# Sending the probabilities of eight head pairs through DRAM instead of TensorE's transposes, with single token tiles and a later branch, in a kernel of attention and two expert layers

## The chip, the cores and the metric

The kernel runs on one core of a Trainium2 chip. The metric is the device time of one execution in microseconds. A core has five engines that work on queues of their own: TensorE (PE; its weight loads are shown as PEld), VectorE (DVE), ScalarE (ACT), GpSimd (POOL) and SyncE (SP), which here issues most DMA transfers. Each engine works through its own instructions in order and waits for the others by semaphores.

## The reference

Three layers run one after another on 4 x 576 = 2304 tokens of 512 features. The first is attention of eight heads in which a query sees itself and the 63 keys before it; the second is a gated layer without experts; the third sends each token to one of eight experts.

```python
scores = scale * np.matmul(q, k.transpose(0, 1, 3, 2))   # 4 x 8 heads, 576 x 576, head size 64
mask = (rel >= 0) & (rel < 64)
attn = np.exp(scores - max); attn = attn / (attn.sum(-1) + 1e-9)
x = np.matmul(attn, v)                                   # -> 2304 x 512
h = ((x @ w1) * (x @ w2)) @ w3 @ w_out                   # 512 -> 1024 -> 512
e_idx = np.argmax(h @ w_gate, axis=1)                    # one of 8 experts per token
for e in range(8):
    mask = e_idx == e
    ye = np.maximum(h[mask] @ ew1[e], 0.0) @ ew2[e]      # 512 -> 1024 -> 512
    out[mask] = gate_w[mask, None] * eom[mask, e, None] * ye
```

## The kernel before

Products in full float32 are made of three passes of a faster format: an operand is split into a high part (ScalarE rounds it) and a low part (VectorE subtracts), and TensorE multiplies high by high, high by low and low by high.

**Attention.** Heads are worked in 16 pairs, n = 0 to 15, four to a batch row. A pair has nine blocks of 64 queries, in three groups g of three blocks. For a group TensorE makes the scores (`score`), VectorE the maximum (`top`), ScalarE the exponentials into a tile p of 128x384 (`exps`), VectorE the reciprocal of the sums (`recip`), and GpSimd multiplies (`normal`). Then TensorE transposes the group's three 128x128 blocks into PSUM (`turn`, tile tps) and ScalarE copies them to SBUF (`keep`, tile PT, one buffer per group). When all three groups are there, TensorE multiplies by v (`pv`, 36 matmuls). Tile p has four buffers.

**Gated layer.** Tokens come in six units u of 384. For each of eight chunks m TensorE makes two gates (`gate`, 12 matmuls each, tile ab), ScalarE and VectorE multiply and split (`keep_a`, `times`, `g_high`, `g_low`), and TensorE multiplies down (`down`, 9 matmuls, tile acc). The products w3 and w_out are multiplied into one matrix beforehand.

**The order.** Up to the end of the gated layer a planner (`Plan.run`) sets the order on every engine. It gets each step with an assumed duration, a rank, the steps that it comes after and the buffers that it takes and gives, and plays it through once while the program is built. The numbers at the head of the file (U0, B2, DB2, ...) set the ranks, that is when a pair or a unit becomes due. On the chip each engine then follows its list and waits where a step isn't ready. Units 2 and 3 are interleaved with pairs 8 to 15.

**Experts.** Each unit's tokens are scattered to a DRAM tensor xs, sorted by expert. Tiles of 128 tokens come back from it. For expert 0 a tile is read in rows and turned by TensorE; for the others it is read in 32-row squares, so that VectorE, which turns squares of 32x32 within a tile, makes the whole turn (`square`), and ScalarE and VectorE split it into exT. The squares of two token tiles share a tile of 1024 columns; there are three of these, used by turns for xg and for expert 0's outputs. Expert 0 begins while the last unit is still being routed; its last token tile (`xg[0, 0]`, worked by `row_block`) waits for that. Ahead of `row_block` stands a branch for more tokens than fit (`row_loop`); with the inputs here it isn't taken. Behind `row_block` comes expert 1 (`static_block`, 96 matmuls into hps), which needs the first three tiles of its tokens.

Of the kernel before, what the change touches and what calls it, by code (L numbers as in the profile page):

```python
# [9 lines left out]
F32 = mybir.dt.float32  # L10
# [12 lines left out]
NP = H // 2  # L23
# [18 lines left out]
U2, DU2, DR = 187.4, 53.25, 6.35  # L42
QO, QS, QE, EN = 5.5, 1.5, -7.3, 359
NEG = -1.0e30
# [89 lines left out]
class Attention:  # L134
# [8 lines left out]
    SUMS = 2 * NP  # L143
    LATE = 2 * NP

    def __init__(self, tc, pool, ps_s, ps_v, qkv, xunit, ident):
# [35 lines left out]
    def exps(self, n, g):  # L182
        nc, s = self.nc, self.s[n]
        ps = s["S", g]
        nm = s.pop(("nm", g))
        p = s["p", g] = self.pool.tile([128, self.GW], F32, name="pp", tag="pp", bufs=PP)
        if n < self.SUMS and g == 0:
            s["rs"] = self.pool.tile([128, 9], F32, name="rs", tag="rs", bufs=3)
        for i in range(3):
            o = slice(128 * i, 128 * i + 128)  # L190
            nc.scalar.activation(out=p[:, o], in_=ps[:, o], func=AF.Exp, bias=nm[:, i:i + 1], scale=0.125,  # L191
                                 **(dict(accum_out=s["rs"][:, 3 * g + i:3 * g + i + 1]) if n < self.SUMS else {}))

    def recip(self, n, g):
        nc, s = self.nc, self.s[n]
        ps = s["S", g]
        if n < self.SUMS:
            a, b = (0, 9) if MERGE else (3 * g, 3 * g + 3)
            rs = s["rs"][:, a:b]
        else:  # L200
            a, b = 0, 3
            rs = ps[:, 392:395]
            nc.vector.tensor_reduce(out=rs, in_=s["p", g].rearrange("p (a b) -> p a b", a=3), axis=AX, op=ALU.add)
        nc.vector.tensor_scalar(ps[:, 400:400 + b - a], rs, 1e-9, None, op0=ALU.add)
        r = self.pool.tile([128, 9], F32, name="r", tag="r", bufs=4)
        nc.vector.reciprocal(out=r[:, 0:b - a], in_=ps[:, 400:400 + b - a])  # L206
        for j in range(3) if b == 9 else (g,):
            s["r", j] = r[:, 3 * j:3 * j + 3] if b == 9 else r[:, 0:3]

    def normal(self, n, g):  # L210
        nc, s = self.nc, self.s[n]
        p = s["p", g].rearrange("p (a b) -> p a b", a=3)
        nc.gpsimd.tensor_tensor(p, p, s.pop(("r", g)).unsqueeze(2).to_broadcast([128, 3, 128]), op=ALU.mult)  # L213

# [13 lines left out]
    def pv(self, n):  # L228
# [4 lines left out]
        for c in range(NB):  # L233
            pv = s["pv"][:, 64 * c:64 * c + 64] if c < 8 else s["pvt"]
            for h in range(2):
                o = 128 * (c % 3) + 64 * h
                nc.tensor.matmul(pv[64 * h:64 * h + 64, :], lhsT=v[:, c, h, :], rhs=s["PT", c // 3][:, o:o + 64],
                                 start=True, stop=True, skip_group_check=True)

# [15 lines left out]
    def plan(self, P, n, r, done):  # L255
# [23 lines left out]
        for g in range(3):  # L279
            q = (-8 if one else -12) + 2 * g  # L280
            add(("nor", g), "POOL", 0.85, q, self.normal, N("rec" if one else ("rec", g)), g)
            add(("tu", g), "PE", 0.36, q, self.turn, N(("nor", g)), g, take=[("S", ("TP", n, g)), (f"PT{g}", ("PT", n, g))],
                give=[("pp", n, g)])
            add(("kp", g), "ACT", 0.5, q, self.keep, N(("tu", g)), g,
                give=[("TP", n, g)])
# [156 lines left out]
def attention_moe_moe_kernel(ctx: ExitStack, tc: tile.TileContext, q0, k0, v, w1, w2, w3, w_out,  # L442
# [29 lines left out]

    s_att, s_exp, s_moe, s_pa, s_mo1, s_ex2, s_ck = [ExitStack() for _ in range(7)]
    E = mybir.EngineType
# [9 lines left out]
    with tc.high_priority():  # L484
# [3 lines left out]
        for _ in range(WARM):  # L488
            mm(cold, lhsT=warm[:, 0:128], rhs=warm, start=True, stop=True)
    att = pool(s_att, "att", side="right")  # L490
    ckp = pool(s_ck, "ck", side="right")

# [8 lines left out]
    with tc.high_priority():  # L501
        at = Attention(tc, att, ps_s, ps_v, (q0, k0, v), xunit, ident)
# [3 lines left out]
    P = Plan(dict(q=2, k=2, v=2, S=2, pv=1, ab=2, acc=UT, pp=PP, PT0=1, PT1=1, PT2=1, ck=RING, f=3, ck2=3,  # L506
                  w3T=3, bits=1, w3p=3, a_sb=2, gt=2, x2=3))
    done = {}
# [214 lines left out]

    def open_exp():
        s_att.close()
        exp_state["p"] = pool(s_exp, "exp", side="right")
# [64 lines left out]

    def pair_tile():
        return exp_state["p"].tile([128, 1024], F32, name="xg", tag="xg", bufs=3)

    def blocks(t, r, n):

        o = t.rearrange("p (j c) -> p j c", c=128)
        for b in range(4):
            nc.sync.dma_start(out=o[32 * b:32 * b + 32],
                              in_=xs[r:r + 128 * n, 128 * b:128 * b + 128].rearrange("(j p) c -> p j c", p=32))  # L800

# [15 lines left out]

    def rows(e, j):

        if j == 0:  # L820
            index_of[e] = index(e)
        t = pair_tile()
        blocks(t, NS * e + 128 * j, 2)
        xg[e, j], xg[e, j + 1] = t[:, 0:512], t[:, 512:1024]

# [363 lines left out]
    def y_first():  # L1189
        if "y" not in hold:  # L1190
            hold["y"] = pair_tile()
            return hold["y"][:, 0:DM]
        return hold["y"][:, DM:2 * DM]

    def rest():

        n0 = nc.values_load(rt.done[0:1, 0:1], min_val=0, max_val=256)
        index(0)
# [24 lines left out]
    def turn(n=1, sp=False):  # L1223
# [4 lines left out]
        for p, t in zip(ps, todo):  # L1228
            halves(p, *t[1:])

    w1e, w2e = eslot(0, 0), eslot(0, 1)
# [8 lines left out]
    written.enter_context(tc.manual_schedule(engines={E.DVE, E.Activation}))  # L1240
    xT_block(xg[0, 0], xT, 0)
    rows(1, 2)
    numbers(1)
    begin(1)
    turn(2)
    row_block(xT, idx[0], 0, w1e, w2e, own, {2: turn})
    for e in range(1, NE):
        at1 = {f: esplit for f in (0, 2, 4, 6)}
        at3 = {1: esplit, 5: esplit}
        if e + 1 < NE:  # L1250
            rows(e + 1, 0)
            rows(e + 1, 2)
# [9 lines left out]
        def tell(label, cond):  # L1262
            tc.mark_branch_hint_location(label, hint=cond, engines={E.PE})

# [72 lines left out]
```

## Time and profile before

| | |
|---|---|
| median of 3 runs | 722.41 us (722.18 to 724.34) |
| the profiled execution, by the same clock | 725.11 us |
| its span, first to last instruction | 723.1 us |
| TensorE busy | 703.1 us, 97% of the span |
| VectorE busy | 393.8 us, 54% |
| ScalarE busy | 307.1 us, 42% |
| GpSimd busy | 151.8 us, 21% |
| mean granted TensorE clock | 0.989 of full speed |

The profile is of one execution, and its stretches add up to its own 723.1 us of span, with 2.0 us around it; the median of the timed runs lies 2.70 us below that execution. Busy shares are means over stages: what a change in a stage is worth is read from the stage.

### The profile page before, as it was taken

Reading aid. Unit: us, or ns where it says so; the run is one execution under the profiler, and the core shown is the slowest. Engines: PE = TensorE matmul, PEld = TensorE weight load, DVE = VectorE, ACT = ScalarE, POOL = GpSimd, SP = SyncE. Lnnn points to the kernel's source line nnn. Section 1 sums busy time; section 2 is a strip of 40 time slices with the busy share of each in tenths; the row PEclk is TensorE's granted clock in tenths of the full one; section 3 lists DMA queues with packets and bytes.
Section 4 is the critical chain, followed back from the end, with each engine's and each line's share of the span. In section 5 each row is a group of like instructions: output and inputs, shape, how many; then the busy total and the mean of one; then the engine's idle time right before and its main releaser. Section 6 shows DMA issues by size and latency. Waiting matters only on the chain. (4 is left out here: it accounts for less than half of the span.)

```text
span 723.1 us, 12045 instructions
## 1 busy us (share of the span) xinstructions
PE 703.1 (97%) x4423; PEld 628.5 (87%) x4423; DVE 393.8 (54%) x882; ACT 307.1 (42%) x707; POOL 151.8 (21%) x183
## 2 busy tenths in 40 slices
PE   6999999999999999999999999988999999999996
PEld 3778899999999999899999999976998998988985
DVE  7899799322654655564531232743756764666210
ACT  3674666322333445343521312542545654555222
POOL 4664654200310221122010010331011001011011
PEclk9899999999999999999999999998999999999999
DMA  8993699960210332120420010667588887474000
GB/s 354 409 365 130 216 299 287 257 156 1 96 52 13 109 125 84 52 83 29 151 69 30 1 44 30 200 180 178 158 229 237 220 239 204 128 223 152 4 29 30
DMA packets 53285, 105.80 MB, mean 146 GB/s; under 512 B 8524, under 2 KB 22860, under 8 KB 53200
## 3 DMA queue, kind: packets, MB, share of 16 engines
q1 hardware_dynamic: 49952, 95.24, 43.0%
q0 software_dynamic: 3104, 9.46, 3.6%
q8 instruction: 45, 0.74, 0.4%
q14 instruction: 40, 0.33, 0.1%
q10 hardware_dynamic: 144, 0.03, 0.0%
HBM read 86.83 MB, written 18.53 MB: 146 GB/s over the span
## 5 line engine op out<-in xcount | busy, mean ns | idle before, releaser
L622 PE MATMUL ab<-xt,w 128*128 128x384 f32 x1152 | 216.4, 340 | 0.0
L622 PEld LDWEIGHTS ab<-xt,w 128*128 128x128 f32 x1152 | 199.5, 188 | 2.1
L646 PE MATMUL acc<-w,gt 128*128 128x512 f32 x432 | 110.4, 400 | 0.0
L1067 PE MATMUL yps<-w,hT 128*128 128x512 f32 x432 | 101.0, 391 | 0.0
L1067 PEld LDWEIGHTS yps<-w,hT 128*128 128x128 f32 x432 | 80.4, 188 | 16.3
L646 PEld LDWEIGHTS acc<-w,gt 128*128 128x128 f32 x432 | 78.8, 188 | 15.2 <-DVE gt L638 0.2
L630 DVE TENSOR_TENSOR a_sb<-ab,a_sb 128x384 f32<-128x384 f32 x48 | 26.7, 556 | 89.8 <-PE ab L622 84.5
L191 ACT ACTIVATE pp<-sps,nm 128x128 f32<-128x128 f32 x144 | 46.8, 366 | 54.2 <-DVE nm L180 50.4
L213 POOL TENSOR_TENSOR pp<-pp,r 128x384 f32<-128x384 f32 x48 | 40.2, 854 | 119.2 <-DVE r L206 83.1
L775 DVE TENSOR_TENSOR w<-ck,w 128x1024 fp32r<-128x1024 f32 x45 | 54.7, 1217 | 12.6 <-ACT w L771 12.2
L1093 PEld LDWEIGHTS hps<-exT,w 128*128 128x128 f32 x384 | 53.6, 197 | 5.3 <-ACT exT L470 3.1
L1093 PE MATMUL hps<-exT,w 128*128 128x288 f32 x384 | 54.8, 305 | 3.6 <-ACT exT L470 2.7
L602 PE MATMUL wps<-w,w3T 128*128 128x512 f32 x192 | 52.5, 419 | 2.3 <-ACT w3T L589 1.3
L771 ACT ACTIVATE w<-ck 128x1024 fp32r<-128x1024 f32 x48 | 50.6, 1056 | 5.5 <-DMA ck<-in_moe_w 4.6
L1059 POOL DMA_INDIRECT out<-y,idx x18 | 17.6, 976 | 161.2 <-ACT y L1058 110.2
L1100 DVE SCALAR_TENSOR_TENSOR hT<-hps,hT 128x256 fp32r<-128x256 f32 x112 | 29.1, 302 | 35.8 <-ACT hT L1098 35.6
L634 ACT ACTIVATE gt<-a_sb 128x384 fp32r<-128x384 f32 x48 | 25.1, 522 | 55.1 <-DVE a_sb L630 55.0
L627 ACT ACTIVATE a_sb<-ab 128x384 f32<-128x384 f32 x48 | 23.6, 492 | 55.2 <-PE ab L622 55.2
L602 PEld LDWEIGHTS wps<-w,w3T 128*128 128x128 f32 x192 | 36.1, 197 | 11.3 <-POOL w3T L593 1.9
L1098 ACT ACTIVATE hT<-hps 128x288 fp32r<-128x288 f32 x56 | 23.1, 412 | 46.9 <-PE hps L1093 43.4
L168 PE MATMUL sps<-k,q 128*128 128x128 f32 x288 | 40.5, 280 | 1.1 <-DMA k<-in_k 1.1
L168 PEld LDWEIGHTS sps<-k,q 128*128 128x128 f32 x288 | 38.0, 194 | 3.9 <-issue 1.7
(155 smaller groups left out, 913.3 us busy)
## 6 DMA issues: line engine op xcount, KB each, us to landing
ck<-in_moe_w SPq DMA_DIRECT2D x80, 512.0 KB, 4.9
q<-in_q SPq DMA_DIRECT2D x16, 576.0 KB, 6.7
v<-in_v SPq DMA_DIRECT2D x16, 576.0 KB, 3.6
xs<-x SPq DMA_DIRECT2D x32, 257.0 KB, 9.6
w<-in_moe_w SPq DMA_DIRECT2D x16, 512.0 KB, 7.4
xg<-xs SPq DMA_DIRECT2D x56, 128.0 KB, 6.2
k<-in_k SPq DMA_DIRECT2D x16, 320.0 KB, 9.6
w<-in_moe_w_out SPq DMA_DIRECT2D x8, 512.0 KB, 7.7
```

Of the source, the lines that this page charges most:

```text
L168: nc.tensor.matmul(ps[:, 128 * i:128 * i + 128], lhsT=s["q"][:, 128 * c:128 * c + 128], rhs=s["k"][:, 64 * c:64 * c + 128], start=late, st ...
L191: nc.scalar.activation(out=p[:, o], in_=ps[:, o], func=AF.Exp, bias=nm[:, i:i + 1], scale=0.125, **(dict(accum_out=s["rs"][:, 3 * g + i:3 ...
L213: nc.gpsimd.tensor_tensor(p, p, s.pop(("r", g)).unsqueeze(2).to_broadcast([128, 3, 128]), op=ALU.mult)
L602: mm(ps, lhsT=t[:, a, 128 * j:128 * j + 128], rhs=wo[b][:, o:o + 512], start=g == 0 and j == 0 and x == 0, stop=g == 1 and j == 3 and x == 2)
L622: mm(ps, lhsT=w[a][:, c:c + 128], rhs=x[:, b, kk, :], start=kk == 0 and i == 0, stop=kk == 3 and i == 2)
L630: V.tensor_tensor(asb[u, m], gps.pop((u, m, 1)), asb[u, m], op=ALU.mult)
L646: mm(accs[u][t], lhsT=g[:, a, 128 * t:128 * t + 128], rhs=ws["w34"][b][:, 512 * m:512 * m + 512], start=m == 0 and i == 0, stop=m == 7 and ...
L771: nc.scalar.activation(out=eparts()[0], in_=eq[0], func=AF.Copy)
L775: low.tensor_tensor(lo, eq.popleft(), hi.bitcast(F32), op=ALU.subtract)
L1067: mm(ps, lhsT=hT[f][a][:, c0:c0 + 128], rhs=w[b][:, 512 * f:512 * f + 512], start=f == 0 and i == 0, stop=f == 7 and i == 2)
L1093: mm(ps[:, 0:W], lhsT=w1e[a][:, c:c + 128], rhs=xT[:, b, kk, 0:W], start=kk == 0 and i == 0, stop=kk == 3 and i == 2)
L1100: nc.vector.scalar_tensor_tensor(out=lo, in0=ps[:, o], scalar=0.0, in1=h[0][:, o].bitcast(F32), op0=ALU.max, op1=ALU.subtract)
```

## The change

It has three parts, and new rank numbers for the planner.

First, for pairs 8 to 15 (`TURN`) the group's probabilities leave in another way. Tile p is laid out by blocks of 32 keys (`by_block`). After `normal`, SyncE writes p to DRAM (`put`, tensor pd) and reads it back in four pieces (`get`, tile xq, two buffers), each of which puts the 32-row squares of one block row in their turned places; VectorE then turns the squares themselves (`flip`), straight into PT. `turn` and `keep` are gone for these pairs, and `pv` reads PT with a stride.

Second, a token tile of the experts is a tile of its own (512 columns, six of them) in place of a half of a pair; reads are issued per tile. Three of expert 1's tiles are read with expert 0's last one, the fourth later.

Third, the branch of expert 0 moves behind `row_block` and gets a hint for TensorE, and GpSimd's order there is written out. The turn of expert 1's third tile moves from the third to the first chunk of `row_block`'s second product.

```diff
-U0, DU0, U1 = 61.9, 11, 134.3
+U0, DU0, U1 = 61.9, 11, 136.8
-B2, DB2, B3, DB3 = 173.4, 16.2, 231.5, 12.2
+B2, DB2, B3, DB3 = 173.2, 13, 231.6, 10.7
...
     def normal(self, n, g):
         nc, s = self.nc, self.s[n]
...
+        if n >= self.TURN:
+            p, r = self.by_block(s["p", g]), r.unsqueeze(3).to_broadcast([128, 3, 4, 32])
...
+    def by_block(self, p):
+        return p.rearrange("p (b k i) -> p k b i", b=4, k=3)
+
+    def put(self, n, g):
+        self.nc.sync.dma_start(out=self.pd[3 * (n % 2) + g], in_=self.s[n].pop(("p", g)))
+
+    def get(self, n, g):
+        t = self.s[n]["Q", g] = self.xq.tile([128, self.GW], F32, name="xq", tag="xq", bufs=2)
+        t = t.rearrange("p (a c) -> p a c", a=4)
+        for b in range(4):
+            self.nc.sync.dma_start(out=t[32 * b:32 * b + 32],
+                                   in_=self.pd[3 * (n % 2) + g][:, 96 * b:96 * b + 96].rearrange("(a p) c -> p a c", p=32))
+
+    def flip(self, n, g):
+        s = self.s[n]
+        PT = s["PT", g] = self.pool.tile([128, self.GW], F32, name="PT", tag=f"PT{g}", bufs=1)
+        self.nc.vector.transpose(out=PT, in_=s.pop(("Q", g)))
...
+                if n >= self.TURN:
+                    PT = PT.rearrange("p (a k j) -> p k a j", a=4, k=3)[:, c % 3, 2 * h:2 * h + 2]
+                    out = out.rearrange("p (a j) -> p a j", a=2)
...
+            if n >= self.TURN:
+                add(("put", g), "DMA", 0.5, q, self.put, N(("nor", g)), g, give=[("pp", n, g)], lat=2.0)
+                add(("get", g), "DMA", 1.8, q, self.get, N(("put", g)), g, take=[("xq", ("xq", n, g))], lat=2.0)
+                add(("kp", g), "DVE", 0.55, q, self.flip, N(("get", g)), g, take=[(f"PT{g}", ("PT", n, g))],
+                    give=[("xq", n, g)])
+                continue
...
-    def pair_tile():
-        return exp_state["p"].tile([128, 1024], F32, name="xg", tag="xg", bufs=3)
+    def square_tile():
+        return exp_state["p"].tile([128, DM], F32, name="xg", tag="xg", bufs=6)
...
-        xg[0, 0] = pair_tile()[:, 0:RW]
-        nc.sync.dma_start(out=xg[0, 0], in_=xs[bass.ds(n0, 128), :])
-        rows(1, 0)
+        xg[0, 0] = square_tile()
+        nc.sync.dma_start(out=xg[0, 0], in_=xs[bass.ds(n0, 128), 0:DM])
+        rows(1, 0, 3)
+        nc.sync.dma_start(out=index_of[0][:, 0, :], in_=xs[bass.ds(n0, 128), DM:RW])
...
-    with tc.If(n > n0 + 128):
-        row_loop(0, n0 + 128, n, w1e, w2e, xT, own)
-    keep_index(0, 0, xg[0, 0])
...
-    rows(1, 2)
+    nc.gpsimd.tensor_copy(idx[0][0][:, 0:1], index_of[0][:, 0, 0:1])
+    rows(1, 3, 4)
...
-    row_block(xT, idx[0], 0, w1e, w2e, own, {2: turn})
+    late = n > n0 + 128
+    row_block(xT, idx[0], 0, w1e, w2e, own, {0: turn, 2: lambda: tell("late", late)})
+    with tc.If(late, label="late"):
+        row_loop(0, n0 + 128, n, w1e, w2e, xT, own)
```

Three places show how the orders move. First SyncE, where pairs 9 to 11 are in work. Before, the queue holds nothing but the pairs' loads.

```order
L156 DMA q<-in_q 128x1152
L156 DMA k<-in_k 128x640
L156 DMA v<-in_v 128x1152 x2
L156 DMA q<-in_q 128x1152
L156 DMA k<-in_k 128x640
```

Now there are the writes to pd and, in fours, the reads of xq among them; the first v below is pair 11's, behind the value matmuls of pair 9, the eight reads are of pair 10's third and pair 11's first group, the next four of its second, the last four of its third.

```order
L228 DMA pd<-pp 128x384
L158 DMA v<-in_v 128x1152
L234 DMA xq<-pd 32x4x96 x8
L228 DMA pd<-pp 128x384
L234 DMA xq<-pd 32x4x96 x4
L158 DMA v<-in_v 128x1152
L234 DMA xq<-pd 32x4x96 x4
```

A read of pair 10's third group stands behind the v load, and behind it are the other pairs' writes and reads.

Second TensorE, from the end of pair 9's value matmuls (pvt) to those of pair 10 (pv). Of the 12 matmuls of a gate (ab) and the 9 of a down (acc) only the first row is shown. Before:

```order
L237 MATMUL pvt<-PT,v 64x64 x2
L622 MATMUL ab<-xt_1195,w_918 128x384 x2
...
L220 MATMUL tps_2745<-ident,pp 128x128 x3
...
L220 MATMUL tps_2755<-ident,pp 128x128 x3
L646 MATMUL acc<-w_577,gt 128x512
...
L168 MATMUL sps<-k,q 128x128 x6
...
L220 MATMUL tps_2892<-ident,pp 128x128 x3
...
L237 MATMUL pv<-PT,v 64x64 x16
```

Now the three turns are gone, and one score group, two gates and one down stand between:

```order
L270 MATMUL pvt<-PT,v 64x64 x2
L170 MATMUL sps<-k,q 128x128 x3
L662 MATMUL ab<-xt_1199,w_1142 128x384 x2
...
L437 MATMUL rps<-oh,tri 128x24
...
L662 MATMUL ab<-xt_1199,w_922 128x384 x2
...
L686 MATMUL acc<-w_581,gt 128x512
...
L270 MATMUL pv<-PT,v 64x64 x16
```

Pair 10's turns are now three of VectorE's instructions instead (L240), the third of them directly ahead of a g_low (L678).

Third SyncE around expert 0's last tile. Before, the load of that tile (L1200) is followed by four reads for expert 1's first two tiles, by three weight loads and the branch (L1236), and only behind the branch by the reads for its third and fourth tile:

```order
L1200 DMA xg<-xs 128x514
L799 DMA xg<-xs 32x8x128 x4
L757 DMA ck_5097<-in_moe_w 128x1024
...
L1236 COMPARE_AND_BRANCH
...
L799 DMA xg<-xs 32x8x128 x4
L803 DMA idx<-xs 128x4x2
L799 DMA xg<-xs 32x8x128 x8
```

Now the twelve reads of expert 1's first three tiles follow at once, and the branch (L1288) comes behind the fourth tile's:

```order
L1238 DMA xg<-xs 128x512
L841 DMA xg<-xs 32x4x128 x12
...
L1240 DMA idx<-xs 128x2
L798 DMA ck_5161<-in_moe_w 128x1024
...
L841 DMA xg<-xs 32x4x128 x4
L845 DMA idx<-xs 128x4x2
L841 DMA xg<-xs 32x4x128 x7
...
L1288 COMPARE_AND_BRANCH
```

## Rows read from the trace of the kernel before

**Rows 1.** The page's first part: busy us (share of the span) xinstructions.
```profile
PE 703.1 (97%) x4423; PEld 628.5 (87%) x4423; DVE 393.8 (54%) x882; ACT 307.1 (42%) x707; POOL 151.8 (21%) x183
```
**Rows 2.** Busy time by stretch: start:end, length, each engine's, granted clock, DMA share, GB/s.
```profile
174.00:345.00 171.00, 171.00 (x1242) 158.77 (x1241) 92.80 (x285) 65.53 (x183) 31.35 (x42) 1.00 0.20 68
...
504.00:508.00 4.00, 4.00 (x18) 4.00 (x18) 0.75 (x3) 1.36 (x2) 0.60 (x2) 0.50 1.02 244
```
**Rows 3.** What TensorE waited for: us in total, times, longest.
```profile
PE hps L1093 <- ACT exT L470: 2.7, 1, 2.7
...
PE hps L1093 <- PEq L1275: 0.4, 1, 0.4
```
**Rows 4.** Timeline, 484 to 503 us: start, length, engine, line, instruction [idle before <-releaser].
```profile
484.91 0.63 PE L845 MATMUL gps<-ident,xg 128*128 128x128 f32 x4 [0.50 <-DMA xg<-xs]
...
486.35 0.60 ACT L470 ACTIVATE exT<-gps 128x512 fp32r<-128x512 f32 x1 [1.16 <-PE gps L845]
...
492.01 0.60 PE L1133 MATMUL tps<-ident,hs 128*128 128x128 f32 x4
...
492.71 0.39 ACT L470 ACTIVATE hT<-tps 128x256 fp32r<-128x256 f32 x1 [1.68 <-PE tps L1133]
...
496.41 1.81 SPq L799 DMA_DIRECT2D xg<-xs  x4
...
501.21 0.73 DVE L854 STREAM_TRANSPOSE gps<-xg 128x512 f32<-128x512 f32 x1 [3.58 <-DMA xg<-xs]
```
**Rows 5.** Timeline of TensorE, the first products of experts 1 and 2.
```profile
502.62 16.13 PE L1093 MATMUL hps<-exT,w 128*128 128x288 f32 x96 [2.70 <-ACT exT L470]
518.58 11.06 PE L1067 MATMUL yps<-w,hT 128*128 128x512 f32 x48
...
533.11 12.96 PE L1093 MATMUL hps<-exT,wx 128*128 128x288 f32 x96
545.91 11.08 PE L1067 MATMUL yps<-w,hT 128*128 128x512 f32 x48
```
**Rows 6.** Groups of instructions, 174 to 345 us: count | busy us, mean ns | idle before.
```profile
L220 PE MATMUL tps<-ident,pp 128*128 128x128 f32 x72 | 11.3, 273 | 0.0
```
**Rows 7.** Timeline of TensorE in attention's second half.
```profile
189.05 2.25 PE L646 MATMUL acc<-w,gt 128*128 128x512 f32 x9
191.14 2.25 PE L622 MATMUL ab<-xt,w 128*128 128x384 f32 x12
193.22 0.49 PE L220 MATMUL tps<-ident,pp 128*128 128x128 f32 x3
193.55 0.83 PE L168 MATMUL sps<-k,q 128*128 128x128 f32 x6
194.14 2.37 PE L622 MATMUL ab<-xt,w 128*128 128x384 f32 x12
...
231.83 1.15 PE L237 MATMUL pv<-PT,v 128*64 128x64 f32 x32
...
233.03 2.37 PE L646 MATMUL acc<-w,gt 128*128 128x512 f32 x9
...
340.77 0.49 PE L220 MATMUL tps<-ident,pp 128*128 128x128 f32 x3
341.01 2.35 PE L646 MATMUL acc<-w,gt 128*128 128x512 f32 x9
```
**Rows 8.** VectorE's turns of token tiles (line 854): count, ns min/median/max, starts.
```profile
L854 DVE STREAM_TRANSPOSE gps<-xg x23: 683/702/727, 488.4 to 702.2; 128x512 f32<-128x512 f32 x23
```
**Rows 9.** Reads of squares by SyncE (line 799): issue in ns, then issue to landing.
```profile
L799 SPq DMA_DIRECT2D xg<-xs x56: 311/443/1618, 482.2 to 649.0; - x56
...
DMA to landing us min/median/max: 3.3/6.2/6.5
```
**Rows 10.** Loads of q, k and v (line 156), 174 to 345 us: issue to landing.
```profile
DMA to landing us min/median/max: 3.6/3.8/4.0
```
**Rows 11.** Reads of token numbers, pieces of 8 bytes (line 803): issue to landing.
```profile
DMA to landing us min/median/max: 4.3/4.6/4.9
```

More of the change, by code (lines that the diff above doesn't have):

```diff
@@ L144, with __init__ @@
     LATE = 2 * NP
-    def __init__(self, tc, pool, ps_s, ps_v, qkv, xunit, ident):
+    TURN = 2 * NP
+    def __init__(self, tc, pool, ps_s, ps_v, qkv, xunit, ident, xq, pd):
+        self.xq, self.pd = xq, pd
         self.tc, self.nc, self.pool, self.ps_s, self.ps_v = tc, tc.nc, pool, ps_s, ps_v
@@ L190, in exps @@
             o = slice(128 * i, 128 * i + 128)
-            nc.scalar.activation(out=p[:, o], in_=ps[:, o], func=AF.Exp, bias=nm[:, i:i + 1], scale=0.125,
+            out, src = p[:, o], ps[:, o]
+            if n >= self.TURN:
+                out, src = self.by_block(p)[:, i], src.rearrange("p (b i) -> p b i", b=4)
+            nc.scalar.activation(out=out, in_=src, func=AF.Exp, bias=nm[:, i:i + 1], scale=0.125,
                                  **(dict(accum_out=s["rs"][:, 3 * g + i:3 * g + i + 1]) if n < self.SUMS else {}))
@@ L202, in recip @@
             rs = ps[:, 392:395]
-            nc.vector.tensor_reduce(out=rs, in_=s["p", g].rearrange("p (a b) -> p a b", a=3), axis=AX, op=ALU.add)
+            nc.vector.tensor_reduce(out=rs, in_=self.by_block(s["p", g]), axis=mybir.AxisListType.XY, op=ALU.add)
         nc.vector.tensor_scalar(ps[:, 400:400 + b - a], rs, 1e-9, None, op0=ALU.add)
@@ L211, in normal @@
         nc, s = self.nc, self.s[n]
-        p = s["p", g].rearrange("p (a b) -> p a b", a=3)
-        nc.gpsimd.tensor_tensor(p, p, s.pop(("r", g)).unsqueeze(2).to_broadcast([128, 3, 128]), op=ALU.mult)
+        r = s.pop(("r", g)).unsqueeze(2)
+        if n >= self.TURN:
+            p, r = self.by_block(s["p", g]), r.unsqueeze(3).to_broadcast([128, 3, 4, 32])
+        else:
+            p, r = s["p", g].rearrange("p (a b) -> p a b", a=3), r.to_broadcast([128, 3, 128])
+        nc.gpsimd.tensor_tensor(p, p, r, op=ALU.mult)
+    def by_block(self, p):
[12 more added lines that the diff above has]
+        self.nc.vector.transpose(out=PT, in_=s.pop(("Q", g)))
     def turn(self, n, g):
@@ L235, in pv @@
             for h in range(2):
-                o = 128 * (c % 3) + 64 * h
-                nc.tensor.matmul(pv[64 * h:64 * h + 64, :], lhsT=v[:, c, h, :], rhs=s["PT", c // 3][:, o:o + 64],
-                                 start=True, stop=True, skip_group_check=True)
+                out, PT = pv[64 * h:64 * h + 64, :], s["PT", c // 3]
+                if n >= self.TURN:
+                    PT = PT.rearrange("p (a k j) -> p k a j", a=4, k=3)[:, c % 3, 2 * h:2 * h + 2]
+                    out = out.rearrange("p (a j) -> p a j", a=2)
+                else:
+                    o = 128 * (c % 3) + 64 * h
+                    PT = PT[:, o:o + 64]
+                nc.tensor.matmul(out, lhsT=v[:, c, h, :], rhs=PT, start=True, stop=True, skip_group_check=True)
     def _x(self, n, tail, i):
@@ L471, in split @@
         low.tensor_tensor(lo, src, hi.bitcast(F32), op=ALU.subtract)
-    s_att, s_exp, s_moe, s_pa, s_mo1, s_ex2, s_ck = [ExitStack() for _ in range(7)]
+    s_att, s_exp, s_moe, s_pa, s_mo1, s_ex2, s_ck, s_xq = [ExitStack() for _ in range(8)]
     E = mybir.EngineType
@@ L490, in attention_moe_moe_kernel @@
     att = pool(s_att, "att", side="right")
+    xq = pool(s_xq, "xq", side="right")
+    pd = dram.tile([6, 128, 384], F32, name="pd")
     ckp = pool(s_ck, "ck", side="right")
@@ L816, in index, with rows @@
         return raw
-    def rows(e, j):
-        if j == 0:
+    def rows(e, j0, j1):
+        if j0 == 0:
             index_of[e] = index(e)
-        t = pair_tile()
-        blocks(t, NS * e + 128 * j, 2)
-        xg[e, j], xg[e, j + 1] = t[:, 0:512], t[:, 512:1024]
+        for j in range(j0, j1):
+            fetch_square(e, j, NS * e + 128 * j)
     def numbers(e):
@@ L1189, in y_first @@
     def y_first():
[L1190 to L1193, printed above, removed]
+        return square_tile()
     def rest():
         n0 = nc.values_load(rt.done[0:1, 0:1], min_val=0, max_val=256)
-        index(0)
-        xg[0, 0] = pair_tile()[:, 0:RW]
-        nc.sync.dma_start(out=xg[0, 0], in_=xs[bass.ds(n0, 128), :])
-        rows(1, 0)
+        index_of[0] = index(0)
+        xg[0, 0] = square_tile()
+        nc.sync.dma_start(out=xg[0, 0], in_=xs[bass.ds(n0, 128), 0:DM])
+        rows(1, 0, 3)
+        nc.sync.dma_start(out=index_of[0][:, 0, :], in_=xs[bass.ds(n0, 128), DM:RW])
     at1 = {k: lambda n=n: step(n) for k, n in {(0, 2): 1, (1, 0): 1, (1, 2): 1, (2, 0): 1, (2, 2): 1, (3, 0): 3, (4, 3): 3, (5, 0): 3}.items()}
@@ L1229, in turn, with tell @@
             halves(p, *t[1:])
+    def tell(label, cond):
+        tc.mark_branch_hint_location(label, hint=cond, engines={E.PE})
     w1e, w2e = eslot(0, 0), eslot(0, 1)
@@ L1250, in attention_moe_moe_kernel @@
         if e + 1 < NE:
-            rows(e + 1, 0)
-            rows(e + 1, 2)
+            rows(e + 1, 0, 4)
             numbers(e + 1)
```

21 lines of the change are left out of this document (11 added, 10 removed).

## The prediction

> **What bounds the kernel now.** I read the page's first part, then the busy time by stretch, then what TensorE waited for. TensorE is busy 97% of the span [rows 1]. In the stretch in which the last eight head pairs are worked, 174 to 345 us, it is busy 171.00 of 171.00 us at full clock, with VectorE at 92.8 us and a DMA share of 0.20 [rows 2]. There a TensorE instruction that is taken out shortens the time, and work put on another engine costs nothing until TensorE has to wait for it. The list of TensorE's waits is short; its longest is 2.7 us, for ScalarE writing exT [rows 3], at the end of expert 0's last token tile.
>
> That 2.7 us wait costs more than its length. Its chain: SyncE issues the load of expert 1's squares 2 and 3 at 496.41 us only, VectorE turns square 2 at 501.21, having waited for that load, and TensorE starts expert 1 at 502.62 [rows 4, 5]. [...] The 96 matmuls that follow took 15.96 us to the start of the next group (502.62 to 518.58); expert 2's 96 took 12.80 (533.11 to 545.91) [rows 5]. So the stall costs 2.70 + 3.16 = 5.86 us.
>
> **Turns taken from TensorE.** 24 groups (8 pairs x 3) of three transposes go, 72 in all, of 273 ns each [rows 6]. They overlap their neighbours, so a duration is not what one costs. I use start to start: a group holds the next row back by 0.33 us in the first row (193.22 to 193.55) and by 0.24 in the last (340.77 to 341.01) [rows 7]; over the 22 rows that hold the 24 groups these distances add up to 6.95 us. Bounds: 6.95 below, and above the busy sum of the stretch's 72, 11.3 us [rows 6]. I take 6.95, since TensorE has no gap there and start to start is what its queue pays. ScalarE loses the 24 copies behind them; it is not the bound, so nothing.
>
> **What comes instead.** VectorE gets 24 turns of 128x384. The nearest row is the 128x512 turn, 702 ns [rows 8]; by size 0.53 us each, 12.6 us, which takes VectorE from 92.8 to 105 of 171 us. Hidden. SyncE gets five issues per group (one write, four reads); issues of that kind take 443 ns [rows 9], so 24 x 5 x 0.44 = 53 us on a queue that until now carries only the pairs' loads. Hidden as issue time, but SyncE works in order: a read waits for its write to land, and the next pair's write, its q, k and v stand behind it. The strided forms of exponential, sum and normalisation, and the strided moving operand of the 36 value matmuls per pair, I cost at nothing: the element counts are the same. The value matmuls are the dangerous one: a pair's 36 take 1.20 us (231.83 to 233.03) [rows 7], 33 ns each; twice that would be 9.6 us over eight pairs. No strided read of that kind stands in the trace; below nothing I see no gain. I take 0.
>
> **When the squares arrive.** PT has one buffer per group and there are two buffers for fetched squares. So of each pair but the first of a burst, the third group is fetched only after the previous pair's value matmuls have ended and its first group has been turned. From that end: turn with its hand-over 0.65, SyncE 0.10, three further issues 1.35, the landing L of the fourth, turn and hand-overs 0.65: 2.75 + L. TensorE has other work meanwhile. In the order printed above, n=10 has a gate, a second one, one down and three scores between the two value groups. A gate is 2.08 and a down 2.09 (189.05 to 191.14 to 193.22), six scores 0.59 [rows 7], so that gap is 6.6 us; counted in the same way, n=9 has 9.3, n=11 11.1, n=13 6.9, n=14 8.4, n=15 6.3. L: the loads of this stage land in 3.6 to 4.0 us [rows 10]; pieces of squares in 3.3 to 6.5 in the busier expert stage [rows 9]; pieces of 8 bytes in 4.3 to 4.9 [rows 11]. With L = 3.3 nothing waits. With 3.8, which I take because it is from the same stage and its light traffic, the chain is 6.55 and only n=15 waits, 0.3 us. With 4.6 n=10, n=13 and n=15 wait 0.75 + 0.45 + 1.05 = 2.25 us.
>
> The read pieces are 384 bytes. [...]
>
> Behind a late third turn on VectorE stands the next g_low, which the down after the value matmuls needs; that down comes later in TensorE's order than the waiting value matmuls, so the wait is not paid twice.
>
> **Expert 0.** With six single tiles expert 1's first three squares are read at once, before the tile in question; only its fourth waits for a buffer. They are 12 issues, some 5.3 us behind 482, and land near 491; square 2 is turned inside the row block, at its first chunk, well before 500. The 2.70 us wait and the 3.16 us of half clock go. ScalarE's exT at 486.35 begins 0.81 us after TensorE's four transposes ended (484.91 + 0.63), right behind the branch; the copy of the next turn follows in 0.10 (492.01 + 0.60 to 492.71) [rows 4]. With the branch moved I take 0.7 off (bounds 0 and 0.8). The branch behind the row block costs TensorE something; the one wait on a hinted branch is 0.4 [rows 3]. I add 0.4 (bounds 0, since no other shows, and 0.8). Single tiles make eight more issues per expert, 3.5 us of SyncE; TensorE waits for no load from 510 us on, so nothing.
>
> **Sum.** On the profiled execution: 725.11 - 6.95 - 2.70 - 3.16 - 0.70 + 0.40 + 0.30 = 712.3 us. The median of the runs lies 2.70 below that execution, so I forecast 709.6 us. This case's own range: 708.5 (no wait, no branch cost) to 712.5 (2.25 of waits, ScalarE no earlier).
>
> **The rivals.**
> *Squares late but harmless otherwise.* L = 6.2, the median of the squares' pieces [rows 9]: chain 8.95, waits 2.35 (n=10) + 2.05 (n=13) + 0.55 (n=14) + 2.65 (n=15) = 7.6: 716.9 us. For it: same kind of transfer. Against: that median is from a stage with far more traffic (DMA share 1.02 in 504 to 508 [rows 2]). 6%.
> *The stall stays* at expert 1's start because something else ends late (the branch on another engine, the third turn): 709.6 + 2.70 + 3.16 = 715.5 us. Against: the row names the load alone, and ScalarE and VectorE idle before it. 7%.
> *Slower: late squares throw the clock down.* If L passes about 6.6 us, n=10 and n=15 wait over 2.7 us, as long as the one wait seen here behind which the clock halved. At L = 7.0 the waits are 0.45 + 3.15 + 2.85 + 1.35 + 3.45 = 11.25 us, three of them with 3.16 behind: 20.7 us on 709.3 (the forecast without waits), 730 us. The point from which it decides is L = 6.6; loads in this stage landed by 4.0 [rows 10]. 5%.
> *The strided read slows the value matmuls to half rate:* 709.6 + 9.6 = 719.2 us. 4%.
> *The turns cost more than their spacing.* With the busy sum of 11.3 [rows 6] in place of 6.95 the time is 705.2 us. The spacings in the rows speak against it. 4%, with what follows. [...]
> My forecast has the remaining 74%.
>
> **Range and chances.** 706 to 717 us holds the forecast and the first two rivals and leaves out the slower one, the half-rate one and the last, 13%, and some tails. A change within 0.3% (2.2 us) can't be told from none here. Slower is the 5% of the clock rival; the same 3%, between it and the half-rate case, whose 719.2 is still 0.4% faster; faster 92%.
>
> **What would show it.** Right: no transposes of pp behind 184 us, TensorE's row of that stretch about 7 us shorter and without waits above 0.5 us; 36 value matmuls of a pair in 1.2 us; the first 96 matmuls of expert 1 in about 12.8 us at clock 1.00, with no wait over 0.5 ahead of them; VectorE's 384-column turn near 0.53 us; reads of pd landing within 4 us. Wrong: TensorE waiting for VectorE's PT at n=10, 13 or 15, a clock below 1.00 in the attention stretch, or a new wait for weights behind 510 us because SyncE's issues are late.

## The result, and the profile after

The changed kernel takes 712.87 us in the median of five runs (711.11 to 713.43), the kernel before 722.41 (721.98 to 724.34) beside it: a ratio of 0.9859, 95% interval 0.9839 to 0.9879. A second measurement of the same kernel (below) gave 0.9862. The profiled execution of the changed kernel took 711.11 us, the shortest of its five. The forecast was 709.6 us, its range 706 to 717.

The page's first part answers to [rows 1]; then follow stretches (as [rows 2]), TensorE's longest waits (as [rows 3]) and its timeline around expert 0's last tile (as [rows 4, 5]).

```profile
PE 693.1 (98%) x4351; PEld 618.3 (87%) x4351; DVE 405.1 (57%) x906; ACT 296.5 (42%) x683; POOL 152.7 (22%) x182
```

```profile
174.00:330.00 156.00, 155.88 (x1132) 144.58 (x1131) 104.04 (x309) 54.16 (x156) 31.24 (x42) 1.00 0.46 135
492.00:496.00 4.00, 4.00 (x32) 4.00 (x31) 2.18 (x5) 1.77 (x3) 0.98 (x1) 1.00 0.58 136
```

```profile
PE sps L166 <- DVE f L616: 1.7, 1, 1.7
PE hps L1134 <- PEq L1319: 1.5, 1, 1.5
...
PE rps L1187 <- ACT exT L508: 0.7, 1, 0.7
PE gps L886 <- DMA xg<-xs: 0.5, 1, 0.5
...
PE hps L1134 <- PEq L1288: 0.2, 1, 0.2
```

```profile
476.65 0.66 PE L886 MATMUL gps<-ident,xg 128*128 128x128 f32 x4 [0.48 <-DMA xg<-xs]
478.04 5.10 PE L1187 MATMUL rps<-wx,exT 128*128 128x512 f32 x18 [0.74 <-ACT exT L508]
...
491.07 12.88 PE L1134 MATMUL hps<-exT,w 128*128 128x288 f32 x96 [0.15 <-PEq L1288]
503.79 11.07 PE L1108 MATMUL yps<-w,hT 128*128 128x512 f32 x48
```

TensorE executes 72 matmuls fewer, and through the last pairs it is still busy all the time at full clock (155.88 of 156.00 us, 1.00). The 2.7 us wait ahead of expert 1 is gone; its 96 matmuls take 12.72 us (491.07 to 503.79) at clock 1.00 where they took 15.96 [rows 5], with 0.50 in 504 to 508 [rows 2]. A wait of 1.5 us is new: it stands ahead of expert 4's first products, at the branch for a few more rows of the expert before it (L1319).

One row serves as a landmark in each part, the same in every kernel: the first small transpose into lps behind 170 us (178.83 before), expert 0's gps, and the yps behind expert 1's 96 matmuls. The distances between their starts, and the share of TensorE's waits in the first, are worked out from the timelines:

| trace of | lps at | lps to gps | of it waits | gps to yps | yps to the end | span |
|---|---|---|---|---|---|---|
| before | 178.83 | 306.08 | 0.75 | 33.67 | 204.52 | 723.1 |
| changed | 178.57 | 298.08 | 0.48 | 27.14 | 205.61 | 709.4 |
| before, again | 177.98 | 306.90 | 1.51 | 32.25 | 204.17 | 721.3 |
| changed, again | 178.23 | 297.72 | 0.72 | 27.06 | 204.79 | 707.8 |
| attention only | 178.32 | 299.02 | 1.59 | 30.19 | 204.77 | 712.3 |
| experts only | 177.29 | 306.33 | 1.15 | 27.29 | 204.19 | 715.1 |
| changed, branch ahead | 177.51 | 298.29 | 1.27 | 27.86 | 204.74 | 708.4 |
| before, branch behind | 178.16 | 306.42 | 1.08 | 27.61 | 204.21 | 716.4 |
| changed, old numbers | 178.24 | 298.44 | 0.98 | 26.78 | 204.64 | 708.1 |

From the first row to the second: 0.26 us at the start, 8.00 in attention, 6.53 at expert 0, and 1.09 lost behind it, together 13.70 of span. The last is this execution's: from the yps to the end the other rows have 204.17 to 204.79. The medians differ by 9.54. That gap, and each term, is what the experiments are about. The theory was the prediction's: TensorE's load falls by the turns, and the stall at expert 1 falls with the single tiles. Its rivals were that the medians' smaller gain is missing in one of the two parts, that the branch and not the tiles removes the stall, and that the new rank numbers make the gain.

### The profile page after: what moved, and what is told of

Its sections match the earlier page's. It is cut to its first block, busy times and chain, and to the rows that moved or that the text cites. A ratio compares the mean times of both kernels' runs of the same rounds, so it can differ in the third digit from the quotient of the medians.

```text
span 709.4 us, 12159 instructions
## 1 busy us (share of the span) xinstructions
PE 693.1 (98%) x4351; PEld 618.3 (87%) x4351; DVE 405.1 (57%) x906; ACT 296.5 (42%) x683; POOL 152.7 (22%) x182
## 5 line engine op out<-in xcount | busy, mean ns | idle before, releaser
L816 DVE TENSOR_TENSOR w<-ck,w 128x1024 fp32r<-128x1024 f32 x45 | 54.6, 1216 | 12.5 <-ACT w L812 12.4
L1134 PEld LDWEIGHTS hps<-exT,w 128*128 128x128 f32 x384 | 50.8, 188 | 2.0 <-issue 1.9
L1134 PE MATMUL hps<-exT,w 128*128 128x288 f32 x384 | 51.5, 294 | 0.7 <-PEq L1314 0.4
```

What stands on the lines that cost most here:

```text
L816: low.tensor_tensor(lo, eq.popleft(), hi.bitcast(F32), op=ALU.subtract)
L1134: mm(ps[:, 0:W], lhsT=w1e[a][:, c:c + 128], rhs=xT[:, b, kk, 0:W], start=kk == 0 and i == 0, stop=kk == 3 and i == 2)
```

## Experiments

Each ratio is against runs of the kernel before on the same chip.

**The kernel before, again.** No edit.

> The kernel before, unchanged, for a second look at its trace. In the profile of before the wait ahead of expert 1 (2.70 us) and the half clock behind it (15.96 instead of 12.8 us for 96 matmuls) stand, and that execution took 725.11 us, 2.70 above the median. Theory A (the 2.70 are ordinary spread): the new trace shows the same wait and the same half clock, whatever its time. Theory B (the shown execution was an unusual one): the wait or the half clock is missing or under half as long in the new trace, whose time is then nearer to 722.4.

Measured: 722.54 us (12 runs, 720.22 to 724.38), ratio 1.0008 (0.9995 to 1.0021). The timeline of the second trace, and two of its stretches:

```profile
484.88 0.63 PE L845 MATMUL gps<-ident,xg 128*128 128x128 f32 x4 [0.30 <-DMA xg<-xs]
...
502.24 0.40 PE L1093 MATMUL hps<-exT,w 128*128 128x288 f32 x1 [1.30 <-ACT exT L470]
502.97 14.32 PE L1093 MATMUL hps<-exT,w 128*128 128x288 f32 x95 [0.33 <-DVE exT L471]
517.13 3.13 PE L1067 MATMUL yps<-w,hT 128*128 128x512 f32 x13
```

```profile
504.00:508.00 4.00, 4.00 (x21) 4.00 (x20) 1.75 (x3) 1.51 (x3) 1.09 (x2) 0.57 0.99 240
508.00:512.00 4.00, 4.00 (x33) 4.00 (x32) 2.23 (x6) 2.03 (x4) 0.00 (x0) 1.00 0.41 131
```

The wait is 1.30 + 0.33 instead of 2.70, and the low clock is over by 508, where the first trace had 0.50 in 504 to 508 [rows 2] and only then recovered. From gps to yps it took 32.25 us, not 33.67. It lies between the two theories: wait and half clock stand in both traces of before, and their size changes.

This trace has a second place of low clock that the first has not. TensorE waits there for ScalarE's exT of expert 0's last tile, ahead of rps, and the clock is 0.50 in 488 to 490:

```profile
487.18 5.98 PE L1146 MATMUL rps<-wx,exT 128*128 128x512 f32 x18 [1.67 <-ACT exT L470]
492.99 0.60 PE L1133 MATMUL tps<-ident,hs 128*128 128x128 f32 x4
```

```profile
488.00:490.00 2.00, 2.00 (x6) 1.60 (x6) 0.77 (x2) 0.01 (x1) 0.00 (x0) 0.50 0.97 365
```

Its 18 matmuls take 5.81 us (487.18 to 492.99), where the changed kernel's take 4.94 (478.04 to 482.98). In the first trace the two waits ahead of rps add up to the same 1.97 us (0.50 + 1.47; here 0.30 + 1.67), and the clock stayed at 1.00.

**Attention only.** The first part of the change with its rank numbers; pairs of tiles and the branch ahead as before.

> Only the attention part of the change (probabilities through DRAM, the new rank numbers); tiles in pairs and the branch ahead, as before. Theory A (both parts give what the two traces show): 8.0 us less, between the last lps group at 178.8 and expert 0's gps, so 714.4 us, and the wait of some 2.7 us ahead of expert 1 with the half clock behind it is still there. Theory B (the three us that the medians lack against the traces are missing here): about 717.5.

Measured: 715.21 us, 0.9915 (0.9899 to 0.9931).

```profile
494.19 0.40 PE L1134 MATMUL hps<-exT,w 128*128 128x288 f32 x1 [1.36 <-ACT exT L508]
494.92 12.77 PE L1134 MATMUL hps<-exT,w 128*128 128x288 f32 x95 [0.32 <-DVE exT L509]
507.53 2.68 PE L1108 MATMUL yps<-w,hT 128*128 128x512 f32 x11
```

Without its waits the stretch to gps is 297.43 us here and 305.33 before, so in this trace the turns' part is whole. By the runs the kernel gains 6.1 us (0.9915) to 6.5 (medians), between the two theories; no trace shows where the rest lies. The stall is there with nearly the same waits as in the run above (1.36 + 0.32), and this time with no half clock behind them: the 95 matmuls take 12.61 us. So in these traces the same wait had no fixed price. The low clock at rps stands here too (0.50 in 480 to 482), and its 18 matmuls take 6.10 us.

**Experts only.** The second and third part of the change on before's attention.

> Only the experts' part of the change (single token tiles, branch behind the row block); attention as before, with its transposes. Theory A: 2.70 (wait) + 3.24 (half clock) + 0.6 (ScalarE earlier, less the branch) go, 1.1 come back as waits for a branch in experts 3 and 4: 5.4 less, 717.0 us, TensorE still has its 72 turns of pp behind 184 us. Theory B (the stall is shorter in before's ordinary executions, and the medians' smaller gain is missing here): about 2 less, 720.

Measured: 717.03 us, 0.9940 (0.9924 to 0.9955). 4.7 us less, where gps to yps is 6.4 us shorter than in the first trace of before and 5.0 shorter than in the second. The 1.1 us of waits at a branch that theory A takes back are not in this trace: behind the yps it takes 204.19, before 204.52. The two parts add up: 0.9915 x 0.9940 = 0.9856, and the whole has 0.9859.

**The changed kernel, again.** No edit.

> The changed kernel itself, for a second look at its trace beside the other runs of this call. Theory A (the 2.70 us by which the shown execution of before lay above its median belonged to the stall at expert 1 and are gone with it; the second trace of before took 32.25 us from expert 0's gps to the yps behind expert 1's 96 matmuls, the first 33.67): this stretch is again near 27.1 us, as in the first trace of the changed kernel, and the time about 10 us below before's median, not 12.8. Theory B (the first trace of the changed kernel was a lucky one in this stretch): over 28.5 us.

Measured: 711.17 us (709.5 to 713.13), 0.9862 (0.9842 to 0.9882), 10.6 us below the median of before. The stretch takes 27.06 us, as theory A says. In all kernels without the stall it lies between 26.8 and 27.9, in those with it between 30.19 and 33.67.

**Branch ahead.** The changed kernel with expert 0's branch where it was.

```diff
+    with tc.If(n > n0 + 128):
+        row_loop(0, n0 + 128, n, w1e, w2e, xT, own)
...
-    row_block(xT, idx[0], 0, w1e, w2e, own, {0: turn, 2: lambda: tell("late", late)})
-    with tc.If(late, label="late"):
-        row_loop(0, n0 + 128, n, w1e, w2e, xT, own)
+    row_block(xT, idx[0], 0, w1e, w2e, own, {0: turn})
```

> The changed kernel with expert 0's branch back ahead of the row block and without its hint; everything else as changed. Theory A (the single tiles took the stall away, by letting expert 1's squares be read earlier): 0.3 to 0.7 us slower, 713.4 us, ScalarE's exT again some 0.8 us behind TensorE's transposes, no wait over 1 us ahead of expert 1, clock 1.00 there. Theory B (the branch's place took it away): the wait and the half clock return, 5.9 slower, 718.8 us.

Measured: 710.89 us, 0.9854 (0.9836 to 0.9871): the same as the changed kernel. No wait ahead of expert 1. The stretch from gps takes 27.86 us, 0.7 to 0.8 more; that is in the trace, and too little for the medians. It is the low clock at rps again (0.50 in 478 to 480): the 18 matmuls take 5.89 us (477.35 to 483.24). All five traces with the branch ahead (the two of before, attention only, turns twice and this one) have 1.95 to 2.16 us of waits ahead of gps and rps, and four of them this low clock, with 5.73 to 6.10 us for the 18 matmuls; in the traces with the branch behind TensorE waits 0.74 us for that exT (0.73 in one), and none has it.

**Branch behind, alone.** The kernel before with the one edit that the branch stands behind `row_block`, hinted.

> The kernel before with one edit: expert 0's branch behind the row block, hinted for TensorE; tiles in pairs, attention as before. Theory A (the single tiles alone take the stall away): TensorE still waits 1.3 to 2.7 us ahead of expert 1, the load of squares 2 and 3 is still issued some 14 us behind the first ones, and the stretch from expert 0's gps to the yps behind expert 1's 96 matmuls takes 29.5 to 33 us: 721.0 us, 0.7 less than before. Theory B (the branch held that load back): no such wait, 27.3 us, 717.

Measured: 717.67 us, 0.9927 (0.9905 to 0.9948), and 27.61 us from gps to yps: theory B in its numbers. SyncE's queue in this kernel, where [rows 4] have the second read of squares at 496.41:

```profile
481.79 1.91 SPq L799 DMA_DIRECT2D xg<-xs  x4
483.79 1.34 SPq L757 DMA_DIRECT2D ck<-in_moe_w  x3
485.30 2.71 SPq L799 DMA_DIRECT2D xg<-xs  x4
...
496.10 4.95 SPq L799 DMA_DIRECT2D xg<-xs  x8
```

What that read waited for in before stands in SyncE's waits, 440 to 505 us:

```profile
SPq L799 <- DMA out<-xg,idx: 10.0, 1, 10.0
```

It waited for the output transfer of expert 0's y, whose buffer it took, and not for the branch, as theory B has it. With the branch behind SyncE still has such a wait (7.3 us), but ahead of the eight reads at 496.10, which are expert 2's. The order of the two programs, with the semaphores of the first of those four reads, agrees: in before (first line) transfers that GpSimd issues (DMASW) and ScalarE are among them, with the branch behind (second line) no such transfer, but TensorE and GpSimd, as the users of expert 0's last tile would be. In the two programs as built those squares lie at the address of expert 0's y (221152) in before, and at that of expert 0's last tile (217056) with the branch behind.

```
L799 DMA xg_5340<-xs_57 32x8x128 [waits DMASW3_49,DMAHW5_49,DMASW2_49,Activation_49]
L799 DMA xg_5213<-xs_57 32x8x128 [waits DMAHW3_49,PE_49,Pool_49]
```

So the single tiles take the stall away without the branch, and the branch takes it away without the single tiles: each hands those squares a buffer that is free earlier. Why the place of the branch changes which of three buffers the tile gets is not settled.

**Turns twice.** The kernel before, each group's transposes of pairs 8 to 15 issued twice.

```diff
-        for i in range(3):
+        for i in [0, 1, 2] * (2 if n >= 2 * NP else 1):
```

> The kernel before with the three transposes of each group of pairs 8 to 15 issued twice, into the same tile: 72 more on TensorE and nothing else. Theory A (a transpose costs its start-to-start distance; six in a row took 0.58 us to the next row in the first half, three 0.24 to 0.33): 6 to 7 us more, 728.5 us. Theory B (it costs its 157 ns share of busy time, 11.3 us for 72): 733. [...]

Measured: 730.92 us, 1.0125 (1.0108 to 1.0143), and a span of 729.2, 7.9 above that of before's second trace. Its timeline:

```profile
195.59 0.82 PE L220 MATMUL tps<-ident,pp 128*128 128x128 f32 x6
196.16 2.33 PE L646 MATMUL acc<-w,gt 128*128 128x512 f32 x9
```

Six hold the next row back by 0.57 us, three by 0.24 (340.77 to 341.01 [rows 7]): 0.33 for three more, 0.11 each. Over the stretch from lps to gps, waits taken out, the 72 cost 313.16 - 305.39 = 7.8 us. Each lasts 273 ns in the profile as before; at that duration as a price the 72 would have cost 19.7. The medians say 9.2; where the other 1.4 lies, no trace shows.

**Eight reads for four.** The changed kernel, each read of a block row cut in two.

```diff
-            self.nc.sync.dma_start(out=t[32 * b:32 * b + 32],
-                                   in_=self.pd[3 * (n % 2) + g][:, 96 * b:96 * b + 96].rearrange("(a p) c -> p a c", p=32))
+            src = self.pd[3 * (n % 2) + g][:, 96 * b:96 * b + 96].rearrange("(a p) c -> p a c", p=32)
+            for o in (0, 16):
+                self.nc.sync.dma_start(out=t[32 * b + o:32 * b + o + 16], in_=src[o:o + 16])
```

> The changed kernel with each read of a block row of squares split into two of 16 partitions: eight issues of SyncE per group instead of four, the same bytes. Four further issues make the chain to the third turn about 1.7 us longer. In the trace of the changed kernel the third turn ends 0.44 us ahead of the value matmuls at 327.05, 0.89 ahead of those at 252.96, 1.40 ahead of those at 309.39. Theory A (these are the margins, and SyncE's issues are what the chain pays): TensorE waits 1.3 + 0.8 + 0.3, 2.4 us slower than the changed kernel, with waits of pv for DVE's PT. Theory B (the planner's order has more room, or landing shrinks as pieces do): under 0.7. Theory C (a late square throws the clock down): over 5 us slower, with a clock under 1.00 behind 320 us.

Measured: 731.30 us, 1.0138 (1.0118 to 1.0158): 20 us slower than the changed kernel. The stretch, TensorE's waits in it, and SyncE's queue:

```profile
174.00:345.00 171.00, 157.00 (x1105) 144.29 (x1103) 100.77 (x304) 53.34 (x153) 31.59 (x42) 0.98 0.40 123
```

```profile
PE pv L271 <- DVE PT L241: 3.3, 2, 2.8
PE sps L170 <- DVE r L211: 2.6, 1, 2.6
PE acc L687 <- DVE gt L679: 2.4, 1, 2.4
```

```profile
320.65 0.37 SPq L228 DMA_DIRECT2D pd<-pp  x1
321.12 4.42 SPq L236 DMA_DIRECT2D xq<-pd  x8
325.63 0.37 SPq L158 DMA_DIRECT2D v<-in_v  x1
326.10 7.79 SPq L236 DMA_DIRECT2D xq<-pd  x16
333.99 0.38 SPq L228 DMA_DIRECT2D pd<-pp  x1
334.47 7.54 SPq L236 DMA_DIRECT2D xq<-pd  x16
```

From 320.65 to 342.01 SyncE issues one transfer after the other. Of theory C the size is right, but the waits come first: 14.75 us of them stand between lps and gps, a stretch that is 20.88 us longer than in the changed kernel; in 174 to 345 us the mean clock is 0.98. The wait for gt is one that the prediction had ruled out as a second payment. VectorE's timeline, with the idle time ahead of an instruction in brackets:

```profile
327.05 0.58 DVE L241 STREAM_TRANSPOSE PT<-xq 128x384 f32<-128x384 f32 x1 [2.33 <-DMA xq<-pd]
327.55 0.52 DVE L679 TENSOR_TENSOR gt<-a_sb,gt 128x384 fp32r<-128x384 f32 x1
```

The g_low of a down stood behind a turn that waited for its squares, and that down stood ahead of the value matmuls. The margin of theory A counted one group's own chain; the next run asks whether the chain or the queue is the limit.

**Four more issues outside a group's own chain.** The changed kernel, four copies of 384 bytes behind each group's reads.

```diff
+        for b in range(4):
+            self.nc.sync.dma_start(out=self.spare[3 * (n - self.TURN) + g, b:b + 1], in_=self.pd[3 * (n % 2) + g][0:1, 96 * b:96 * b + 96])
```

> The changed kernel with four tiny copies more behind each group's four reads, 384 bytes each from DRAM to DRAM, which nothing waits for: as many issues of SyncE as in the run with eight reads, but none within a group's own chain. Theory A (the 20 us of the run with eight reads come from SyncE's time per pair: issue after issue in order, 13.4 us per pair where pairs follow in 8 to 10): TensorE waits again, 8 to 20 us slower than the changed kernel, some 720 to 731. Theory B (they come from the longer chain of each group's own reads): at most one set of tiny issues stands ahead of a third group, 1.7 us, so under 2.4 us slower, 713.

Measured: 739.75 us, 1.0232 (1.0205 to 1.0259): 27 us slower than the changed kernel, more than theory A said. An issue of these copies took longer than a read's (median 587 ns against 430; columns: least, median, most):

```profile
L237 SPq DMA_DIRECT2D spare<-pd x96: 467/587/1475, 189.3 to 354.2; - x96
```

```profile
PE acc L690 <- DVE gt L682: 5.9, 3, 2.7
PE rps L439 <- DVE xt L287: 3.7, 1, 3.7
```

So SyncE's queue is the limit, and not only the chain of a group's own reads. The run does not show that issue time alone does it, for the copies are not quite free of others: SyncE also waited ahead of two of them for loads of v to land (3.2 us), and the profile names copies as what two of GpSimd's products waited for (15.8 us). How much of the 27 us comes from that is not separated. In issue time a pair costs SyncE three writes of 0.34 us, twelve reads of 0.43 and three loads of about 0.4, 7.4 us in the changed kernel; 12.4 with eight reads; 14.4 here. TensorE's two longest waits, shown above, are not for PT but for a g_low and a split of x, VectorE's work too.

**Old numbers.** The changed kernel with before's ten rank numbers.

> The changed kernel with the rank numbers of before (U1, B2, DB2, B3, DB3, U2, DU2, DR, QO, QE); all three parts of the change stay. Theory A (what TensorE no longer does is the gain, and the numbers only place it): from the lps at 178 to expert 0's gps 297.2 us without waits, and waits of under 3 us in all: 711 to 714 us. Theory B (the new numbers make the squares come in time): TensorE waits over 5 us for PT, 718 or more, with half clock behind the long ones.

Measured: 709.83 us, 0.9836 (0.9809 to 0.9864), with 0.98 us of waits from lps to gps. The gain is there without the new numbers; it is, if anything, larger than theory A's 711 to 714.

**Earlier hint**, twice. The changed kernel, experts 1 to 7.

```diff
-        at2.update({7: lambda: tell(f"lots{e}", reg["lots"])})
+        at2.update({3: lambda: tell(f"lots{e}", reg["lots"])})
```

> The changed kernel with the hint for the branch of experts 1 to 7 given at the fourth chunk of the second product instead of the eighth. In its trace TensorE waited 1.5 us at expert 4's branch (hps behind PEq), 0.4 at another. Theory A (the hint comes too late for the code behind the branch to be there): no wait over 0.3 us at these branches, some 1.5 us faster than the changed kernel. Theory B (the wait has another cause): the same time, and such a wait at one of the branches again.

> The changed kernel with the earlier hint in experts 1 to 7 once more, as it was the fastest so far, 0.9827 of before against 0.9859 and 0.9862 for the changed kernel. Theory A (the earlier hint is worth what TensorE's waits at the branches of experts 2 and 4 are longer without it, 0.2 to 1.1 us): 0.984 to 0.986. Theory B (it is worth the whole 2.5 us): 0.982 to 0.983.

Measured: 708.64 us, 0.9827 (0.9809 to 0.9844), and 709.23, 0.9817 (0.9793 to 0.9840). The second trace has the wait again:

```profile
PE hps L1134 <- PEq L1319: 1.3, 1, 1.3
```

So theory A of the first run falls: that wait (1.5 in the first trace of the changed kernel, 0.6 in the second, 0.4 and 1.3 here) is at the branch for `few_rows`, which carries no hint, and the hint that was moved belongs to another branch. Twice the version came out 0.3 to 0.4% faster than the changed kernel, with intervals that overlap; no trace shows where, and it stays open whether the gain is real. Of all kernels here it is the fastest.

## Why the prediction was right

The bound, the three gains and the direction held. One slip in its adding: by the terms that it names its own narrow range is 708.9 to 712.2 us, not 708.5 to 712.5. By its own steps:

**TensorE's turns: right, mis-sized.** 6.95 us were forecast, 8.0 measured. The start-to-start distances of the turns do add up to that, but a block of wide matmuls behind a small kind ran longer than one behind another wide block. In the second trace of before:

```profile
188.20 2.25 PE L646 MATMUL acc<-w,gt 128*128 128x512 f32 x9
190.29 2.25 PE L622 MATMUL ab<-xt,w 128*128 128x384 f32 x12
...
195.50 0.49 PE L220 MATMUL tps<-ident,pp 128*128 128x128 f32 x3
195.74 2.34 PE L646 MATMUL acc<-w,gt 128*128 128x512 f32 x9
197.92 2.25 PE L622 MATMUL ab<-xt,w 128*128 128x384 f32 x12
```

A down behind a gate took 2.09 us (188.20 to 190.29), behind a turn 2.18 (195.74 to 197.92). With that a turn costs 0.33 us or a little more, 24 of them 8.0, and the run with doubled turns gives the same 0.33.

**What comes instead: right.** VectorE's turn took 578 ns (0.53 forecast). A pair's 36 value matmuls took 1.20 us (327.05 to 328.25), as in before (231.83 to 233.03 [rows 7]), so the strided read cost nothing here.

```profile
327.05 1.15 PE L270 MATMUL pv<-PT,v 128*64 128x64 f32 x32
...
328.25 2.37 PE L686 MATMUL acc<-w,gt 128*128 128x512 f32 x9
```

**The squares' arrival: L too long, the limit in another place.** L was taken as 3.8 us; the reads of squares landed so:

```profile
DMA to landing us min/median/max: 1.7/2.5/4.4
```

No value matmul waited; the closest third turn ended 0.44 us ahead of them (326.03 + 0.58 to 327.05). So the 0.30 is 0, and the reads in 384-byte pieces landed, in the median, sooner than those in 8-byte pieces, 4.3 to 4.9 [rows 11]; the slowest passed the 4 us that the prediction set. The loads of q, k and v, from which 3.8 was taken, move 320 to 576 KB each, a read of squares 48, so they were no near row. No run here reads these squares in longer pieces, so what the length of a piece costs this layout is not shown. The rival "slower" named the right place and the wrong quantity: it put the point of decision at a landing of 6.6 us. The two runs with more issues show it in SyncE's time per pair. Between its last two value matmuls the changed kernel has 7.66 us (319.39 to 327.05) for the 7.4 us of a pair's issues. By this sum the margin is small, but the queue is not full there: SyncE's last reads are issued by 322.41 (317.19 + 5.22). "The wait is not paid twice" was wrong in the run with eight reads, where a down waited ahead of the value matmuls.

**The stall at expert 1: right in what it costs this execution, half right in the cause.** 2.70 + 3.16 were forecast; in the profiled executions 2.70 and 3.24 went. The single tiles suffice, as the prediction says; the moved branch alone suffices as well, which it did not see.

**ScalarE's exT and the branch.** 0.70 forecast, 0.70 measured (rps 2.09 us behind gps before, 1.39 now). What the prediction could not see in its one trace is the low clock behind that wait, some 0.9 us in the other traces with the branch ahead (the 18 matmuls of rps took 5.73 to 6.10 us in them, 4.94 in the changed kernel). The branch cost TensorE 0.15 us where 0.40 was put.

**The step that did not hold is the last one, "minus 2.70".** On the profiled execution the sum was 712.3 us, and that of the changed kernel took 711.11. But the distance of before's profiled execution from its median was carried over as if it had nothing to do with the change. The stretch with the stall took 33.67 us in that execution, 32.25 in the second one of before and 30.19 in the attention-only kernel, and these two hold the low clock at rps besides. So 1.4 us or more of such a distance can be the stall itself, which goes with the change, and the prediction then took it off twice.

That is not the whole gap between traces and medians. The changed kernel's two profiled executions lie 1.76 and 1.67 us below their own medians, where before's lay above, and no trace shows why. Both parts are worth less by the runs than in the traces: the experts' part 4.3 us (0.9940) where the sum had 6.2, the attention part 6.1 (0.9915) where the trace has 7.9. Had the offset been left out, the forecast would have been 712.3 beside a measured 712.87, but that closeness would be luck in part: a sum 1.2 us too high for the profiled execution meets a median 1.76 above it.

## What to carry to other kernels

The stall with a clock drop behind it had a different size in each execution here: the stretch around it took 33.67 and 32.25 us in the two traces of before. When the profiled execution lies above the median (here by 2.70 us), part of that distance can be the stall, so a change that removes it should not be credited with its profiled size and with the median's distance as well. A second trace of the kernel before shows how far the stall varies, and may show one that the first has not, as here the 0.50 at rps. Moving work from a saturated engine to transfers was priced here by the issuing queue's time per round (7.4 us of issues where pairs follow in 7.7; with 12.4 and 14.4 us the kernel was 20 and 27 us slower), not only by one chain's latency. And an in-order engine behind a late transfer delayed its other customers as well: with eight reads VectorE idled 2.33 us ahead of a turn, and TensorE waited 2.4 us for the g_low behind it. Before crediting the new buffers, find out which buffer the late load takes and what frees it: two unrelated edits may remove the same wait, as the single tiles and the moved branch did here (27.86 and 27.61 us from gps to yps, 33.67 and 32.25 in before).

## What the runs showed of the hardware

Equal waits of TensorE had unequal consequences: behind 1.30 + 0.33 us the granted clock was 0.57 over the 4 us of 504 to 508, behind 1.36 + 0.32 it stayed at 1.00, and behind 2.70 it was 0.50 in 504 to 508. The same 1.97 us in two waits ahead of rps left it at 1.00 in one trace of the kernel before and was followed by 0.50 in the other. A block of nine or twelve wide matmuls took 2.09 us behind another block of wide matmuls and 2.17 to 2.18 behind small transposes. A transpose of 128x128 lasted 273 ns in the profile and cost 0.11 us of TensorE's time in a row of its kind (six held the next row back by 0.57 us, three by 0.24). Issuing a copy of 384 bytes from DRAM to DRAM took SyncE 587 ns in the median, a read of 12,288 elements into SBUF 428.
